# Three centred-only tiles instead of two, one of them in column halves of its product, with all loads on one queue and a newly searched order

## The chip, the cores and the metric

One core of a Trainium2 chip. The rounds ran on several chips (the first comparison on one, e1 to e8 on a second, e9 to e11 on a third, e12 and e13 on a fourth), and each ratio compares runs of the same rounds. The metric is device microseconds of one execution, median of several runs. The span, from the first to the last instruction in a profile, is about 1.3 us shorter than that time. All runs compared here are fast ones with a granted TensorE clock of 1.0.

## The reference

```python
# x: (1, 2048, 512) bf16; w1, w2: (512, 512); w3: (512, 1792); w4: (1792, 512)
h  = gelu(layernorm(x) @ w1)
hs = concat([shift(h_j, s) for h_j, s in zip(split(h, 4), (1, -1, 2, -2))]) @ w2   # zero padded along tokens
x1 = x + hs
out = x1 + gelu(layernorm(x1) @ w3) @ w4
```

## The kernel before

Tokens lie in 16 tiles of 128 rows; in the names, tiles 16 to 31 are those of x1, the input of the second layer norm. A small recording layer collects operations with their reads and writes, a list scheduler in the kernel's source puts them in an order for each engine, and semaphores are derived from that order. Layer 1 needs layernorm(x) with the channels on partitions, so each normalised tile is transposed, by TensorE (`ty`, `sa`/`sb` in the script) or by a DMA transpose. Then 128-column "up" products give h with channels on partitions, ready for the mixing product.

The first two tiles take another path, "centred only" (`NAT`). Only the mean is subtracted before the transpose; the product is made with the tokens on partitions ("rows"), where 1/sigma can be a per-partition scale of the GELU, and h is transposed back (`th`). So TensorE can start before `rstd` (1/sigma) is known.

```python
GROUPS = {1: (1, 1, 1, 1, 1, 1, 2, 2, 2, 2, 2), 2: (2, 2, 4, 4, 4)}
NORM = {4: "act", 5: "act", ...}          # engine of a tile's normalisation; default VectorE
NAT = (0, 1)                              # centred-only tiles
SPLIT = (0,)                              # ... centred and transposed in column halves
LOADS = """
x0 w1a w1b x4-5 w2b tp2 x3 w2a x6-7 w3b x8 w3a x1@act x9 x2@act x11 tp16 w4a x10 tp11 w4b tp9 x12-14 x15
"""
SCRIPT = """
warm:8 sa:0 sb:0 ty:1 ra:0 rb:0 up1:1 ty:2 th:0-1 up1:2 mix:0 ty:4 ty:3 mix:1 up1:3 ty:5 up1:4 mix:2 up1:5
mix:3 ty:17 mix:4 up2:0 up1:6 up2:1 mix:6 down:1 mix:5 up1:7-8 ...
"""

# in ln(): a centred-only tile
if t in SPLIT:
    for hh in (0, 1):
        cs = slice(hh * D // 2, (hh + 1) * D // 2)
        pg.add(how, f"norm{q}_{hh}", ... e.tensor_scalar(dst[:, cs], src[:, cs], mv[:, q, 0:1], None, ALU.subtract))

# in mm_up_rows(t): the product with tokens on partitions
if t in SPLIT:
    for hh in (0, 1):                     # halves of the sum over channels: first half needs w1a and half of x only
        pg.add("pe", f"rows{t}_{hh}", part(2 * hh, 2 * hh + 2), ...)
        if hh == 0:
            yield
pg.add("act", f"gelur{t}",
       lambda e: e.activation(hn[:, k, :], y_ps[:, p, 0:D], ACT_F.Gelu_apprx_tanh, scale=rstd[:, t : t + 1]), ...)

# in ln(), at its end: tiles that TensorE does not transpose
if q not in pe_tp:
    pg.add("sp", f"tp{q}",
           lambda e: e.dma_start(xT[:, :, P * t : P * (t + 1)], xn_buf[:, slot(q), :], transpose=True), ...)
```

`GROUPS` says how many tiles each block of up products takes, for layers 1 and 2. In `LOADS`, `w1a` is the first half of w1, `x4-5` one transfer of two tiles, `@act` a load issued from ScalarE's queue; everything else is issued by SyncE in this order, with the DMA transposes and the stores.

Of the kernel before, what the change touches and what calls it, by code (L numbers as in the profile page):

```python
# [6 lines left out]
P = 128  # L7
# [18 lines left out]
class Program:  # L26
# [5 lines left out]
    DUE = 252723.0  # L32
# [225 lines left out]
GROUPS = {1: (1, 1, 1, 1, 1, 1, 2, 2, 2, 2, 2), 2: (2, 2, 4, 4, 4)}  # L258
NORM = {4: "act", 5: "act", 6: "act", 10: "act", 11: "pool", 12: "pool", 13: "act", 15: "act", 18: "pool", 20: "pool", 21: "pool", 22: "pool", 24: "act", 28: "act", 30: "pool"}
EVAC = {1: "both", 2: "dve", 3: "dve", 7: "both", 9: "dve", 10: "both", 11: "both", 13: "both", 16: "dve", 17: "both", 19: "both", 20: "dve", 22: "both", 23: "dve", 24: "dve", 25: "dve", 28: "dve", 31: "dve"}  # L260
STAT_ACT = (1, 6, 8, 9, 12, 21, 22, 23, 27, 28, 29)
TAIL = (256, 128, 128)
NMR = {0: "pool", 1: "pool", 3: "pool", 5: "pool", 7: "pool", 9: "pool", 10: "pool", 12: "pool", 13: "pool", 14: "pool", 17: "pool", 18: "pool", 19: "pool", 21: "pool", 22: "pool", 23: "pool", 27: "pool", 30: "pool"}
NAT = (0, 1)
SPLIT = (0,)
HEV = {2: "dve", 5: "dve", 6: "dve"}
BIAS = {}
LOADS = """
x0 w1a w1b x4-5 w2b tp2 x3 w2a x6-7 w3b x8 w3a x1@act x9 x2@act x11 tp16 w4a x10 tp11 w4b tp9 x12-14 x15
"""  # L270
SCRIPT = """
warm:8 sa:0 sb:0 ty:1 ra:0 rb:0 up1:1 ty:2 th:0-1 up1:2 mix:0 ty:4 ty:3 mix:1 up1:3 ty:5 up1:4 mix:2 up1:5
mix:3 ty:17 mix:4 up2:0 up1:6 up2:1 mix:6 down:1 mix:5 up1:7-8 mix:8 mix:7 up1:9 mix:10 down:0 down:2 mix:9
up1:10 mix:12 mix:11 up2:2 mix:13 down:3 down:6 mix:14 up2:3 mix:15 down:4-5 down:7 down:11 down:9-10 up2:4
down:8 down:12 down:14 down:13 down:15
"""

def bass_standalone__mixer_s_mlp__prompt_kernel(nc, x, w1, w2, w3, w4, out):
# [14 lines left out]
    with ExitStack() as es:  # L293
# [37 lines left out]
        def pair_rv(p, v):  # L331
            return [(("y", p, 0), v), (("y", p, 1), v)]
# [180 lines left out]
        def mm_up_rows(t):  # L513
# [11 lines left out]

            if t in SPLIT:
# [7 lines left out]
            else:  # L534
# [6 lines left out]
                   reads=pair_rv(p, v) + [(("rstd", t), 0), (("warm",), 1)], writes=[(("hn", t), 0)], dur=50 + D * 0.833)  # L541
            yield

        def h_transpose(t, pair):
            g = group_of[1, t]
            how = HEV.get(t, "act")
            k = NAT.index(t)
            if pair:
                b, v = next_pair()
                res, dst = pair_rv(b, v), y_bf[:, b, 0:D]  # L550
            else:
                b, v = next_bank()
                res, dst = [(("o", b), v)], o_bf[:, b, 0:D]

            def f(e):
                for c in range(DC):
                    ins = e.transpose(dst[:, P * c : P * (c + 1)], hn[:, k, P * c : P * (c + 1)], ident[:])  # L557
                return ins

            pg.add("pe", f"th{t}", f, reads=[(("hn", t), 0), (("ident",), 1)], writes=res, dur=225)  # L560
            to, frm = hT[:, :, 2 + P * t : 2 + P * (t + 1)], dst.rearrange("p (c s) -> p c s", s=P)
            pg.add(how, f"evh{t}",
                   (lambda e: e.activation(to, frm, ACT_F.Copy)) if how == "act" else
                   (lambda e: e.tensor_copy(to, frm)),
                   reads=res, writes=[(("h", j, g), 0) for j in range(DC)],
                   dur=(60 + 0.82 * D) if how == "act" else (75 + 0.51 * D))

# [37 lines left out]
        def run(gen):  # L605
            for _ in gen:
                pass
# [81 lines left out]
        steps = []  # L689
# [4 lines left out]
        steps = [s for s in steps if s[0] not in ("th", "tz") or s[1] in NAT]  # L694
# [13 lines left out]
        for kind, n in steps:  # L708
            if kind == "warm":
                warm_pe(n)  # L710
            elif kind in ("sa", "ra"):
# [118 lines left out]
```

## Time and profile before

| | before |
|---|---|
| time, median (range) | 135.71 us (135.43 to 135.89) |
| profiled span | 134.6 us |
| TensorE busy | 130.6 us |
| first TensorE wait on data | 0.4 us on w1, at 5.6 us |

How to read the views: a chain line is start, length, what; it follows the last instruction back to what released it. A wait line is engine, line and tile of the waiter, what it waited for, total us, times, longest. A timeline line is start, length, engine, line, operation, output and inputs, count. L586 (L619 after the change) are the up products, L655 (L688) the down products, L626 (L659) the mixing products, L520 and L534 the row products, L482 (L483) transposes of x, L557 (L587) transposes of h. PSUM is the buffer that TensorE writes; ScalarE or VectorE must empty a part of it before it is used again.

### The profile page before, as it was taken

To read this page: it belongs to the slowest core of one execution; us is meant where nothing else is said; L and a number is where in the kernel's file an instruction comes from. 1 tells how busy PE (TensorE), PEld (TensorE's weight loads), DVE (VectorE), ACT (ScalarE), POOL (GpSimd) and SP (SyncE) were. 2 spreads that over 40 slices of the span, in tenths; PEclk is the share of its full clock that TensorE was granted. 3 is DMA by queue.
4 is the path that set the end of the run, shared out by engine and by line. 5 is a ranking of instruction groups with operands and counts; after the bars stand their busy time and mean duration, and the time that the engine had idled before them with its cause. 6 is when DMAs were issued, how large, how long until landed. Compare 5 with 4: busy or idle time off the path is not lost.

```text
span 134.6 us, 2013 instructions
## 1 busy us (share of the span) xinstructions
PE 130.6 (97%) x780; PEld 72.7 (54%) x792; DVE 52.1 (39%) x140; ACT 58.5 (44%) x90; POOL 25.9 (19%) x59
## 2 busy tenths in 40 slices
PE   8889999999999999999999999999999999999994
PEld 3467688886586446444444444444444444444463
DVE  3779999403947627700053500062222200012222
ACT  6598995768484402775530366500000155520000
POOL 2533467600865301200010310010000000000000
DMA  6999398599056532111003110003111100001112
GB/s 198 298 381 380 80 294 161 98 271 271 0 117 82 118 78 78 39 39 39 5 0 78 39 39 0 0 0 85 39 39 65 52 0 0 0 5 39 39 39 78
DMA packets 21897, 12.32 MB, mean 92 GB/s; under 512 B 14464, under 2 KB 21376, under 8 KB 21888
## 3 DMA queue, kind: packets, MB, share of 16 engines
q1 hardware_dynamic: 21168, 11.80, 32.9%
q10 hardware_dynamic: 720, 0.39, 1.0%
q8 instruction: 6, 0.10, 0.3%
q14 instruction: 3, 0.02, 0.0%
HBM read 6.82 MB, written 2.10 MB: 66 GB/s over the span
## 4 chain that ended last, share of the span: by engine, by line
PE 93%; DMA 4%; issue 1%; SPq 1%; ACT 1%; DVE 0%; ACTq 0%
PE y_ps L586 45%; PE o_ps L655 36%; PE o_ps L626 10%; DMA w_sb<-in_w_dram 4%; PE y_ps L520 1%; PE y_ps L482 1%; ACT hn L539 1%; SPq L372 0%; PE o_ps L557 0%; SPq L365 0%; DVE o_sb L663 0%; ACTq L779 0%; SPq L815 0%
## 5 line engine op out<-in xcount | busy, mean ns | idle before, releaser
L586 PE MATMUL y_ps<-xnT,w_sb 128*128 128x256 bf16 (+2 forms) x421 | 62.4, 306 | 0.2
L586 PEld LDWEIGHTS y_ps<-xnT,w_sb 128*128 128x128 bf16 x424 | 39.0, 98 | 23.4 <-DVE xnT L490 0.3
L655 PE MATMUL o_ps<-w_sb,h2T 128*128 128x512 bf16 (+2 forms) x247 | 49.0, 355 | 0.3
L601 ACT ACTIVATE h2T<-y_ps 128x1024 bf16<-128x1024 f32 (+1 forms) x29 | 28.6, 994 | 42.6 <-PE y_ps L586 42.6
L655 PEld LDWEIGHTS o_ps<-w_sb,h2T 128*128 128x128 bf16 x252 | 23.6, 98 | 25.2
L663 DVE TENSOR_TENSOR o_sb<-o_ps,x_sb 128x512 bf16<-128x512 f32 (+2 forms) x18 | 11.4, 633 | 40.0 <-PE o_ps L655 39.8
L416 POOL TENSOR_TENSOR rstd<-mv,neghalf 128x1 f32<-128x1 f32 x21 | 11.7, 555 | 42.8 <-DVE mv L411 38.7
L626 PE MATMUL o_ps<-w_sb,hT 128*128 128x512 bf16 x60 | 15.2, 379 | 0.3
L409 DVE BATCH_NORM_STATS2 st<-x_sb 128x6 f32<-128x512 bf16 x21 | 14.2, 676 | 2.1 <-DMA x_sb<-in_x_dram 1.8
L637 DVE TENSOR_TENSOR x_sb<-o_ps,x_sb 128x512 bf16<-128x512 f32 x10 | 6.9, 687 | 12.7 <-PE o_ps L626 12.7
L633 DVE SCALAR_TENSOR_TENSOR x_sb<-o_ps,x_sb 128x512 bf16<-128x512 f32 x6 | 4.1, 690 | 16.8 <-PE o_ps L626 16.7
L601 ACT ACTIVATE hT<-y_ps 128x1024 bf16<-128x1024 f32 (+1 forms) x9 | 7.4, 827 | 6.3 <-PE y_ps L586 6.2
L416 POOL TENSOR_TENSOR rstd<-vpe,neghalf 128x1 f32<-128x1 f32 x11 | 6.0, 551 | 18.8 <-DVE vpe L405 18.7
L626 PEld LDWEIGHTS o_ps<-w_sb,hT 128*128 128x128 bf16 x64 | 6.0, 98 | 5.5
L437 DVE TENSOR_SCALAR xn_buf<-x_sb,mv,rstd 128x512 bf16<-128x512 bf16 x15 | 7.0, 469 | 4.9 <-POOL rstd L416 4.6
L446 ACT ACTIVATE xn_buf<-x_sb,nmr,rstd 128x512 bf16<-128x512 bf16 x8 | 6.5, 813 | 5.1 <-DVE nmr L442 3.2
L393 ACT ACTIVATE junk<-x_sb 128x512 bf16<-128x512 bf16 x11 | 6.9, 624 | 2.7 <-DVE x_sb L633 2.7
L449 POOL TENSOR_SCALAR xn_buf<-x_sb,rstd,nmr 128x512 bf16<-128x512 bf16 x7 | 5.4, 768 | 0.8 <-DVE nmr L442 0.4
L679 PE MATMUL o_ps<-zeros 128*128 128x512 bf16 x8 | 3.6, 631 | 0.6 <-POOLq L815 0.6
L411 DVE BATCH_NORM_AGGREGATE mv<-st 128x2 f32<-128x9 f32 x21 | 4.0, 191 | 0.2
L388 ACT ACTIVATE junk<-x_sb 128x512 bf16<-128x512 bf16 x5 | 3.1, 625 | 0.2 <-DMA x_sb<-in_x_dram 0.2
L482 PEld LDWEIGHTS y_ps<-ident,xn_buf 128*128 128x128 bf16 x28 | 2.3, 111 | 1.3 <-issue 0.5
(35 smaller groups left out, 30.5 us busy)
## 6 DMA issues: line engine op xcount, KB each, us to landing
w_sb<-in_w_dram SPq DMA_DIRECT2D x4, 896.0 KB, 6.8
out_dram<-o_sb SPq DMA_DIRECT2D x15, 128.0 KB, 1.7
w_sb<-in_w_dram SPq DMA_DIRECT2D x4, 256.0 KB, 5.2
x_sb<-in_x_dram SPq DMA_DIRECT2D x7, 128.0 KB, 5.2
x_sb<-in_x_dram SPq DMA_DIRECT2D x2, 256.0 KB, 5.5
xnT<-xn_buf SPq DMA_TRANSPOSE x25, 2.5
x_sb<-in_x_dram SPq DMA_DIRECT2D x1, 384.0 KB, 6.0
x_sb<-in_x_dram ACTq DMA_DIRECT2D x2, 128.0 KB, 3.0
```

The source lines that it names most:

```text
L393: (lambda d: (lambda e: e.activation(d, src, ACT_F.Square, accum_out=sums[:, q, 1:2])))(junk[:, b, :]),
L409: pg.add("dve", f"bnst{q}", lambda e: e.bn_stats(st9[:, q, 0:6], src), reads=rs, writes=[(("st", q), 0)], dur=605)
L416: lambda e: e.tensor_tensor(col(rstd), var, neghalf[:], ALU.pow),
L437: lambda e: e.tensor_scalar(dst, src, mv[:, q, 0:1], rstd[:, q : q + 1], ALU.subtract, ALU.mult),
L446: f = lambda e: e.activation(dst, src, ACT_F.Identity, bias=nmr[:, q : q + 1], scale=rstd[:, q : q + 1])
L449: f = lambda e: e.tensor_scalar(dst, src, rstd[:, q : q + 1], nmr[:, q : q + 1], ALU.mult, ALU.add)
L586: ins = e.matmul(y_ps[:, p, W * i : W * (i + 1)], wsb[:, dc, P * fc : P * (fc + 1)], src[:, dc, P * t0 : P * t0 + W], start=(dc == 0), sto ...
L601: (lambda d, s: (lambda e: e.activation(d, s, ACT_F.Gelu_apprx_tanh)))(dst, ysrc),
L626: ins = e.matmul(dst, hT[:, j, c0 : c0 + P], w2_sb[:, j, :], start=(j == 0), stop=(j == DC - 1))
L637: f = lambda e: e.tensor_tensor(x1_sb[:, t, :], dst, x_sb[:, t, :], ALU.add)
L655: ins = e.matmul(dst, h2T[:, fc, P * t : P * (t + 1)], w4_sb[:, fc, cs], start=(fc == 0), stop=(fc == FC - 1))
L663: (lambda d, c: (lambda e: e.tensor_tensor(o_sb[:, oi, c], d, x1_sb[:, t, c], ALU.add)))(dst, cs),
```

## The change

The intent is to fill TensorE's early idle time: a third tile takes the centred-only path, so that more products are ready before the first rstd; tile 1 is split in halves like tile 0 and its products interleaved with tile 0's; the third tile's product is made in two column halves, so that its first GELU starts earlier. Groups, engines of the side work, loads and script were searched anew, with loads that land late assumed in the search.

```diff
-GROUPS = {1: (1, 1, 1, 1, 1, 1, 2, 2, 2, 2, 2), 2: (2, 2, 4, 4, 4)}
+GROUPS = {1: (1, 1, 1, 1, 1, 1, 2, 2, 2, 4), 2: (2, 4, 4, 4, 2)}
+NORM = {1: "pool", 5: "pool", 7: "pool", ...}            # new table; 14 full tiles and tile 1 on GpSimd
-NAT = (0, 1)
-SPLIT = (0,)
+NAT = (0, 1, 2)
+SPLIT = (0, 1)
+CSPLIT = (2,)
-x0 w1a w1b x4-5 w2b tp2 x3 w2a x6-7 w3b x8 w3a x1@act x9 x2@act x11 tp16 w4a x10 tp11 w4b tp9 x12-14 x15
+tp16 x0-1 x2 x3 w1a w1b x4-5 w2b w2a x6 x7-9 tp2 x12 x10-11 w3b w3a w4a w4b x14 x15 tp8 x13
-warm:8 sa:0 sb:0 ty:1 ra:0 rb:0 up1:1 ty:2 th:0-1 up1:2 mix:0 ...
+warm:9 sa:0 sb:0 sa:1 sb:1 ty:2 ra:0-1 rb:0-1 ra:2 ty:3 th:0 rb:2 th:1 up1:3 ta:2 tb:2 mix:0 ty:4 mix:1 ty:5
+up1:4 mix:2 up1:5 ty:16 mix:3 ty:17 mix:4 up2:0 up1:6 down:0 up1:7 ...
+            if t in CSPLIT:                              # in mm_up_rows
+                for hh in (0, 1):
+                    cs = slice(H * hh, H * (hh + 1))
+                    ... 4 products of 256 columns into one half of y_ps, then gelur{t}_{hh} on that half
+                    yield
 (... h_transpose does a CSPLIT tile in two halves in the same way ...)
```

`tp16` and `tp2` in the new list do nothing, because TensorE transposes these tiles.

More of the change, by code (lines that the diff above doesn't have):

```diff
@@ L31 @@
     LOOK = {"dve": 300.0, "act": 300.0}
-    DUE = 252723.0
+    DUE = 414330.0
     BEGIN = {"sp": 30.0, "act": 150.0, "pe": 400.0, "dve": 150.0, "pool": 450.0}
@@ L256, in place @@
         return out
-GROUPS = {1: (1, 1, 1, 1, 1, 1, 2, 2, 2, 2, 2), 2: (2, 2, 4, 4, 4)}
-NORM = {4: "act", 5: "act", 6: "act", 10: "act", 11: "pool", 12: "pool", 13: "act", 15: "act", 18: "pool", 20: "pool", 21: "pool", 22: "pool", 24: "act", 28: "act", 30: "pool"}
-EVAC = {1: "both", 2: "dve", 3: "dve", 7: "both", 9: "dve", 10: "both", 11: "both", 13: "both", 16: "dve", 17: "both", 19: "both", 20: "dve", 22: "both", 23: "dve", 24: "dve", 25: "dve", 28: "dve", 31: "dve"}
-STAT_ACT = (1, 6, 8, 9, 12, 21, 22, 23, 27, 28, 29)
+GROUPS = {1: (1, 1, 1, 1, 1, 1, 2, 2, 2, 4), 2: (2, 4, 4, 4, 2)}
@@ L262 @@
+NORM = {1: "pool", 5: "pool", 7: "pool", 8: "pool", 9: "pool", 10: "pool", 11: "act", 15: "act", 16: "act", 18: "pool", 19: "pool", 20: "act", 22: "pool", 23: "pool", 24: "pool", 26: "pool", 27: "pool", 28: "pool", 29: "pool", 30: "act"}
+EVAC = {0: "dve", 3: "dve", 5: "dve", 9: "both", 10: "both", 11: "both", 14: "both", 15: "dve", 16: "dve", 17: "both", 18: "dve", 19: "dve", 23: "both", 24: "both", 25: "both", 27: "dve", 30: "dve"}
+STAT_ACT = (1, 2, 8, 12, 13, 18, 24, 26, 27, 29, 31)
 TAIL = (256, 128, 128)
-NMR = {0: "pool", 1: "pool", 3: "pool", 5: "pool", 7: "pool", 9: "pool", 10: "pool", 12: "pool", 13: "pool", 14: "pool", 17: "pool", 18: "pool", 19: "pool", 21: "pool", 22: "pool", 23: "pool", 27: "pool", 30: "pool"}
@@ L264 @@
-NAT = (0, 1)
-SPLIT = (0,)
-HEV = {2: "dve", 5: "dve", 6: "dve"}
+NMR = {2: "pool", 3: "pool", 5: "pool", 6: "pool", 8: "pool", 12: "pool", 14: "pool", 17: "pool", 18: "pool", 20: "pool", 22: "pool", 29: "pool", 30: "pool", 31: "pool"}
+NAT = (0, 1, 2)
+SPLIT = (0, 1)
+CSPLIT = (2,)
+HEV = {3: "dve"}
 BIAS = {}
 LOADS = """
-x0 w1a w1b x4-5 w2b tp2 x3 w2a x6-7 w3b x8 w3a x1@act x9 x2@act x11 tp16 w4a x10 tp11 w4b tp9 x12-14 x15
+tp16 x0-1 x2 x3 w1a w1b x4-5 w2b w2a x6 x7-9 tp2 x12 x10-11 w3b w3a w4a w4b x14 x15 tp8 x13
@@ L270 @@
 """
 SCRIPT = """
-warm:8 sa:0 sb:0 ty:1 ra:0 rb:0 up1:1 ty:2 th:0-1 up1:2 mix:0 ty:4 ty:3 mix:1 up1:3 ty:5 up1:4 mix:2 up1:5
-mix:3 ty:17 mix:4 up2:0 up1:6 up2:1 mix:6 down:1 mix:5 up1:7-8 mix:8 mix:7 up1:9 mix:10 down:0 down:2 mix:9
-up1:10 mix:12 mix:11 up2:2 mix:13 down:3 down:6 mix:14 up2:3 mix:15 down:4-5 down:7 down:11 down:9-10 up2:4
-down:8 down:12 down:14 down:13 down:15
+warm:9 sa:0 sb:0 sa:1 sb:1 ty:2 ra:0-1 rb:0-1 ra:2 ty:3 th:0 rb:2 th:1 up1:3 ta:2 tb:2 mix:0 ty:4 mix:1 ty:5
+up1:4 mix:2 up1:5 ty:16 mix:3 ty:17 mix:4 up2:0 up1:6 down:0 up1:7 mix:5 down:1 mix:6 up1:8 mix:8 mix:7
@@ L276 @@
+up1:9 mix:9-10 up2:1 mix:13 mix:12 up2:2 mix:11 down:3 down:7 down:4 mix:14 up2:3 mix:15 down:2 down:6
+down:11 down:8 down:12 up2:4 down:10 down:5 down:9 down:14 down:13 down:15
 """
@@ L524, in part, with f @@
                 return f
+            if t in CSPLIT:
+                H = D // 2
+                for hh in (0, 1):
+                    cs = slice(H * hh, H * (hh + 1))
+                    def f(e, hh=hh, cs=cs):
+                        for dc in range(DC):
+                            ins = e.matmul(y_ps[:, p, 512 * hh : 512 * hh + H], xnT[:, dc, P * t : P * (t + 1)],
+                                           w1_sb[:, dc, cs], start=(dc == 0), stop=(dc == DC - 1))
+                        return ins
+                    pg.add("pe", f"rows{t}_{hh}", f,
+                           reads=[(("w1", c), 0) for c in range(DC)] + [(("xT", t, c), 1) for c in range(DC)],
+                           writes=[pair_rv(p, v)[hh]], dur=DC * 109.2)
+                    pg.add("act", f"gelur{t}_{hh}",
+                           (lambda a, b: (lambda e: e.activation(a, b, ACT_F.Gelu_apprx_tanh,
+                                                                 scale=rstd[:, t : t + 1])))(
+                               hn[:, k, cs], y_ps[:, p, 512 * hh : 512 * hh + H]),
+                           reads=[pair_rv(p, v)[hh], (("rstd", t), 0), (("warm",), 1)], writes=[(("hn", t, hh), 0)],
+                           dur=50 + H * 0.833)
+                    yield
+                return
             if t in SPLIT:
@@ L540, in mm_up_rows, with h_transpose @@
                                           scale=rstd[:, t : t + 1]),
-                   reads=pair_rv(p, v) + [(("rstd", t), 0), (("warm",), 1)], writes=[(("hn", t), 0)], dur=50 + D * 0.833)
+                   reads=pair_rv(p, v) + [(("rstd", t), 0), (("warm",), 1)],
+                   writes=[(("hn", t, hh), 0) for hh in (0, 1)], dur=50 + D * 0.833)
             yield
-        def h_transpose(t, pair):
+        def h_transpose(t):
             g = group_of[1, t]
@@ L547, in h_transpose @@
             k = NAT.index(t)
-            if pair:
+            if t in CSPLIT:
                 b, v = next_pair()
-                res, dst = pair_rv(b, v), y_bf[:, b, 0:D]
+                steps = [(2 * hh, 2 * hh + 2, [pair_rv(b, v)[hh]], f"_{hh}") for hh in (0, 1)]
+                dst = y_bf[:, b, :].rearrange("p (k x) -> p k x", k=2)[:, :, 0 : D // 2]
+                chunk = lambda c: dst[:, c // 2, P * (c % 2) : P * (c % 2 + 1)]
+                part = lambda c0, c1: dst[:, c0 // 2, :].rearrange("p (c s) -> p c s", s=P)
@@ L551, in h_transpose @@
             else:
                 b, v = next_bank()
-                res, dst = [(("o", b), v)], o_bf[:, b, 0:D]
-            def f(e):
-                for c in range(DC):
-                    ins = e.transpose(dst[:, P * c : P * (c + 1)], hn[:, k, P * c : P * (c + 1)], ident[:])
-                return ins
-            pg.add("pe", f"th{t}", f, reads=[(("hn", t), 0), (("ident",), 1)], writes=res, dur=225)
-            to, frm = hT[:, :, 2 + P * t : 2 + P * (t + 1)], dst.rearrange("p (c s) -> p c s", s=P)
@@ L562, in h_transpose @@
-            pg.add(how, f"evh{t}",
-                   (lambda e: e.activation(to, frm, ACT_F.Copy)) if how == "act" else
-                   (lambda e: e.tensor_copy(to, frm)),
-                   reads=res, writes=[(("h", j, g), 0) for j in range(DC)],
-                   dur=(60 + 0.82 * D) if how == "act" else (75 + 0.51 * D))
+                steps = [(0, DC, [(("o", b), v)], "")]
+                dst = o_bf[:, b, 0:D]
+                chunk = lambda c: dst[:, P * c : P * (c + 1)]
+                part = lambda c0, c1: dst.rearrange("p (c s) -> p c s", s=P)
@@ new lines, in h_transpose, with f @@
+            for c0, c1, res, tag in steps:
+                def f(e, c0=c0, c1=c1):
+                    for c in range(c0, c1):
+                        ins = e.transpose(chunk(c), hn[:, k, P * c : P * (c + 1)], ident[:])
+                    return ins
+                n = c1 - c0
+                pg.add("pe", f"th{t}{tag}", f,
+                       reads=[(("hn", t, hh), 0) for hh in range(c0 // 2, c1 // 2)] + [(("ident",), 1)],
+                       writes=res, dur=56 * n if n < DC else 225)
+                to, frm = hT[:, c0:c1, 2 + P * t : 2 + P * (t + 1)], part(c0, c1)
+                pg.add(how, f"evh{t}{tag}",
+                       (lambda a, b: (lambda e: e.activation(a, b, ACT_F.Copy)) if how == "act" else
+                        (lambda e: e.tensor_copy(a, b)))(to, frm),
+                       reads=res, writes=[(("h", j, g), 0) for j in range(c0, c1)],
+                       dur=(60 + 0.82 * n * P) if how == "act" else (75 + 0.51 * n * P))
+                yield
@@ L693, in bass_standalone__mixer_s_mlp__prompt_kernel @@
             steps += [(kind, n) for n in (range(int(a), int(b or a) + 1) if kind != "warm" else [int(n)])]
-        steps = [s for s in steps if s[0] not in ("th", "tz") or s[1] in NAT]
+        steps = [s for s in steps if s[0] != "th" or s[1] in NAT]
         pe_tp = {n for kind, n in steps if kind in ("tp", "ty", "sa")}
@@ L710, in bass_standalone__mixer_s_mlp__prompt_kernel @@
                 warm_pe(n)
-            elif kind in ("sa", "ra"):
-                halves[kind[0], n] = pe_transpose(n, n, True) if kind == "sa" else mm_up_rows(n)
+            elif kind in ("sa", "ra", "ta"):
+                halves[kind[0], n] = {"s": lambda n: pe_transpose(n, n, True), "r": mm_up_rows,
+                                      "t": h_transpose}[kind[0]](n)
                 next(halves[kind[0], n])
-            elif kind in ("sb", "rb"):
+            elif kind in ("sb", "rb", "tb"):
                 next(halves[kind[0], n])
@@ L717, in bass_standalone__mixer_s_mlp__prompt_kernel @@
                 run(pe_transpose(n % NT, n, kind == "ty"))
-            elif kind in ("th", "tz"):
-                h_transpose(n, kind == "tz")
+            elif kind == "th":
+                run(h_transpose(n))
             elif kind == "mix":
```

## The prediction

> **What bounds the kernel now.** I read the page's busy shares and its row of forty slices first, then the chain of work that ended last in order of time, then the waits of TensorE, and last the instructions of the first 18 us one by one.
>
> ```profile
> span 134.6 us, 2013 instructions
> PE 130.6 (97%) x780; PEld 72.7 (54%) x792; DVE 52.1 (39%) x140; ACT 58.5 (44%) x90; POOL 25.9 (19%) x59
> ...
> PE   8889999999999999999999999999999999999994
> ...
> DVE  3779999403947627700053500062222200012222
> ```
>
> TensorE is full in every slice from the fourth on; VectorE is nearly full in slices 4 to 6 only (10 to 20 us), so it can set the pace only there. The share of 97% flatters: it counts warm-up products on zeros and products at half clock. The chain says more:
>
> ```profile
> 0.99 5.01 DMA w_sb<-in_w_dram
> ...
> 6.04 1.48 PE y_ps L520 x6
> ...
> 7.61 0.70 ACT hn L539
> ...
> 8.35 0.40 PE o_ps L557 x4
> 8.75 0.89 PE y_ps L586 x16
> ...
> 17.58 13.97 PE y_ps L586 x128
> ...
> 132.73 0.02 issue
> ```
>
> The columns are start, length, what. Until 6.0 us the end hangs on the second half of w1 landing; at 7.6 on one GELU; from 8.35 us to 132.7 on TensorE alone, product after product. The 128 products of 256 columns from 17.58 us take 109 ns each, so there is nothing to win in the body, unless products are removed, and the sum of columns is not changed. TensorE's waits confirm it; there are three in the whole run:
>
> ```profile
> PE o_ps L679 <- POOLq L815: 0.6, 1, 0.6
> PE y_ps L520 <- DMA w_sb<-in_w_dram: 0.4, 1, 0.4
> PE o_ps L557 <- ACT hn L539: 0.4, 1, 0.4
> ```
>
> **Idle ledger, before.** I take the start of the first 256-column block of layer 2, 17.58 us, as the mark; both kernels have the same kinds of work before it. Useful TensorE work before the mark, from start-to-start spacings in the trace (215.8 ns for 512 columns, 55.6 ns for 128): 8 row products 1.73, 36 transposes 2.00, 64 up products of 128 columns 3.56, 20 mix products 4.32; sum 11.60 us. Lost: 17.58 - 11.60 = 5.98 us. Nearly all lies before 8.35 us. Only this can shrink.
>
> **What the Trainium skill says.** (1) "TensorE: Matmul & The Clock Gate", Part 1, gives 106.7 and 426.7 ns between starts of 128- and 512-column products while cold, 55.6 and 215.7 ns warm, and a change about 4 us into activity. The trace agrees: the warm-up products start every 427 ns from 0.64 us, transposes at 4.03 us are still 107 ns apart, and from about 4.8 us on the spacing is the warm one. (2) "DMA: Bandwidth & Descriptors", Queues, rings and completion order, says each DMA engine takes turns between the queue rows it has work for, by packet. The trace's packets show this: x2, issued from ScalarE, moves between 2.8 and 3.3 us while SyncE's queue nearly stops, and the w1 half behind it reaches ten engines at 4.3 to 4.6 us, the other six at 5.3 to 6.0. (3) "GPSIMD Engine Reference", specification table, says GpSimd shares its SBUF interfaces with VectorE. The trace agrees:
>
> ```profile
> 19.57 0.77 POOL L449 TENSOR_SCALAR xn_buf<-x_sb,rstd,nmr 128x512 bf16<-128x512 bf16 x1
> 19.68 0.80 DVE L437 TENSOR_SCALAR xn_buf<-x_sb,mv,rstd 128x512 bf16<-128x512 bf16 x1 [0.24 <-POOL rstd L416]
> ```
>
> VectorE's normalisation takes 0.41 us when alone, 0.80 us beside GpSimd's. (4) The table at the head of "TensorE: Matmul & The Clock Gate" also says that ScalarE and VectorE take instructions strictly in order; no row of this trace goes against it, and it matters for the new order below.
>
> **The change part by part.**
> *Work.* Tile 2 leaves the 128-column path (16 products of 55.6 ns, 0.89 us) for 8 row products of 256 columns (8 x 109 = 0.87 us) and gains 4 transposes of its product. Tile 16 (the first x1 tile) is transposed on TensorE instead of by DMA: 4 more. So +8 transposes, +0.44 us. One layer-1 group of four tiles replaces two of two: 16 products fewer, at 2.3 ns of fixed spacing each, -0.04 us. A ninth warm-up product fills time that nothing else could use.
> *Loads.* All x loads now go through SyncE's queue; x0 and x1 are one transfer; x2 and x3 stand before w1. So 1024 KB instead of 896 KB precede the end of w1. In the trace the queue moves about 344 KB per us once running (84 to 90 KB per 250 ns); with no turn-taking dip I estimate x0-1 at 2.7 us, x2 3.05, x3 3.4, w1 halves at 4.2 and 5.0. Before they were x0 2.4, w1 3.9 and 6.0.
> *The new head*, by hand from the trace's durations and the order in each engine's program. Nine warm-up products end at 0.64 + 9 x 0.427 = 4.46 us. Tile 0: bn_stats 2.72, aggregate 3.45, halves subtracted from 3.68 on. Tile 1's halves go to GpSimd from 3.52, about 0.5 us each (between its 0.27 for one column and 0.77 for 512); VectorE beside it is slowed, but still ahead of TensorE. Twelve transposes: four cold, the rest warm, done at 5.3. VectorE empties tile 0's first half at 4.91, then its program has bn_stats of tile 3 (about 0.6 us to the next start), then the second half at 5.73 to 6.02. The interleave covers this: first halves of tiles 0 and 1 at 5.29 and 5.72, second halves at 6.15 and 6.59, then tile 2's first column half 7.02, tile 3's transposes to 7.67. GELU of tile 0 comes after a ScalarE sum of squares and ends at 7.81, so the product's transposes wait 0.19. Then second column half, transposes and up products of tile 3 follow with no gap to 9.85. ScalarE must run, in this order, GELU 0, GELU 1, half GELU 2, copy 0, half GELU 2, copy 1: 7.12 + 3 x 0.6 + 0.38 x 2 + 0.6 gives 10.3 us, so mix 0 waits 0.45.
> From there: 5 mixes 4.32, tiles 4 and 5 1.78, transposes of tiles 4, 5, 16, 17 0.89: 10.3 + 6.99 = 17.3. VectorE's copy for tile 17 ends at about 17.25 by the same reckoning, so it is just in time. **Mark at 17.35 us.**
> *Ledger, after:* work 11.60 - 0.89 + 0.87 + 0.44 = 12.03 (rounded); lost 17.35 - 12.03 = 5.32 us. The head loses 0.66 us less, pays 0.43 us more work: the mark moves by -0.23 us. With -0.04 us later: **-0.27 us**. The tail (three column pieces of the last tile) is unchanged, and the last layer-2 block, now two tiles wide, is followed by down products of other tiles first, as before, so its GELUs stay hidden. 135.56 - 0.27 = 135.3; I lean 0.1 us lower, because the order was searched and my hand order takes every wait at full. **135.2 us.**
>
> **Rivals.**
> A. *The loads bite.* If six DMA engines fall behind again (1 to 1.4 us in this trace), w1's second half lands at about 6.4, row products slip 0.3 us and the gain is gone: about 135.5. Against it: one queue, no turn-taking.
> B. *Transposes by DMA wait behind the weights.* Before, tiles 6 and 7 were transposed between w4's halves; now all of w3, w4, x14 and x15 (about 6.5 MB) are queued ahead. At the rates above they end at about 20.4 us; tile 7's transpose then lands at about 21.7. It is needed at 17.35 + 56 x 0.109 = 23.5 us. A margin of 1.8 us; if the queue is slower by a tenth it is used up, and TensorE would stand for up to 1 us: 136.2.
> C. *VectorE or ScalarE becomes the bound from 8 to 18 us.* VectorE is nearly full there; GpSimd has 14 full normalisations where it had 7 (and tile 1's halves), each able to stretch a VectorE pass by 0.4 us. Two such on the path make the mark 18.1: 136.0.
> D. *The head shrinks more than I reckon*: if ScalarE's copies are quicker and mix 0 does not wait, 0.6 us better: 134.6.
> E. *All of it hidden*: the same waits in other places, 135.6.
>
> **Range and chances.** The whole loss that could be removed is 5.98 us, of which 4.1 us pass before the clock is warm, so 2% (2.7 us) faster is hardly possible. Slower by 2% needs B or C several times over. D and C set the range: 134.3 to 136.1. Faster 0.03, same 0.94, slower 0.03.
>
> **What would show it.** TensorE's waits: none on w1 above 0.2 us; one on a GELU or a ScalarE copy of h before mix 0, 0.2 to 0.5 us. The chain: w1 no longer its first long piece, but VectorE or ScalarE pieces between 5 and 10 us. The first 56 products of 256 columns starting at 17.0 to 17.7 us. No wait on a DMA transpose at 23 us. The second half of w1 landing near 5 us. I am wrong if TensorE has a wait of over 0.3 us after the mark, or if the mark lies outside 16.7 to 18.2 us.

## The result

| | before | after |
|---|---|---|
| time, median of 4 runs | 135.71 us (135.43 to 135.89) | 137.43 us (136.78 to 137.76) |
| ratio | | 1.0123 (95%: 1.0076 to 1.0169) |
| profiled span | 134.6 us | 135.4 us (the fastest of the four) |
| first layer-2 block starts ("the mark") | 17.41 us | 17.84 us |
| last product starts | 132.49 us | 133.37 us |
| time between the two | 115.08 us | 115.52 us |

A ratio here is the mean time of one kernel's fast runs over that of the other's of the same rounds, so it is not quite the ratio of the medians. The changed kernel is slower, by 1.2%, still within 2%, but outside the range of 134.3 to 136.1.

The last three rows come from the trace's record of each product. The prediction read the mark of the kernel before as 17.58 us; that is where the chain's piece begins, which is when the product ahead of it is modelled to end. The first product of the block was issued at 17.41.

The page of the changed kernel:

```profile
span 135.4 us, 2007 instructions
PE 131.9 (97%) x777; PEld 71.1 (53%) x777; DVE 52.3 (39%) x142; ACT 56.7 (42%) x89; POOL 32.6 (24%) x67
...
PE   8899999999999999999999999999999999999994
...
DVE  2879999865764700070004144001522220030422
```

GpSimd has 6.7 us more work and VectorE no less. Nothing else on this page tells why the time is longer. TensorE's waits do:

```profile
PE o_ps L712 <- POOLq L849: 0.6, 1, 0.6
PE y_ps L483 <- POOL xn_buf L428: 0.6, 1, 0.6
PE y_ps L619 <- ACT h2T L634: 0.3, 1, 0.3
```

The waits for w1 and for the GELU are gone, as intended. In their place stands one for GpSimd at the start and one before an up product. The chain of the same run places both:

```profile
0.09 2.78 DMA x_sb<-in_x_dram
...
4.78 0.96 POOL xn_buf L428
...
5.78 0.30 PE y_ps L483 x2
...
6.98 0.62 ACT junk L394 x2
...
7.85 0.62 DVE st L410
...
17.96 5.31 PE y_ps L619 x48
23.27 0.02 issue
23.29 1.03 ACT h2T L634
24.33 0.12 issue
24.45 1.91 PE y_ps L619 x16
```

From 24.45 us on, the chain is TensorE without a break, as in the kernel before. The second wait is attributed to a GELU that ended at 24.32 us. But the up products at 24.45 us (layer 1, tiles 6 and 7) don't read that GELU's result, and the PSUM pair that they write had been emptied by an earlier GELU. What they do read is xnT of tile 7, whose DMA transpose landed at 24.31 us by the trace's landing records. Two releases ended within 10 ns, and the profile chose one. A second profile of the same kernel, below, names the other.

The first wait, seen in the timeline of the changed kernel:

```profile
3.80 1.92 POOL L428 TENSOR_SCALAR xn_buf<-x_sb,mv 128x256 bf16<-128x256 bf16 x2 [2.10 <-ACT junk L389]
3.85 0.70 DVE L428 TENSOR_SCALAR xn_buf<-x_sb,mv 128x256 bf16<-128x256 bf16 x2
4.47 0.47 DVE L434 TENSOR_SCALAR xn_buf<-x_sb,mv 128x512 bf16<-128x512 bf16 x1
```

The two half passes of tile 1 on GpSimd take 0.99 and 0.95 us (0.98 from start to start), where I had put about 0.5 us each. VectorE does such a half in 0.29 us when alone (3.38 us in the kernel before).

The loads, by the trace's landing records (us; all 16 engines done):

| | x0 | w1, 2nd half | w3, all | w4, all | x15 | tile 6 transposed | tile 7 transposed |
|---|---|---|---|---|---|---|---|
| before | 2.40 | 6.00 | 14.21 | 30.44 | - | 21.52 | 22.83 |
| after, estimated | 2.7 | 5.0 | - | - | 20.4 | - | 21.7 |
| after, measured | 2.87 | 6.66 | 16.05 | 21.64 | 22.40 | 22.88 | 24.31 |

SyncE's queue in the changed kernel shows how the transposes come to stand behind the loads:

```profile
10.69 5.19 SPq L366 DMA_DIRECT2D x_sb<-in_x_dram  x2
...
19.04 3.87 SPq L456 DMA_TRANSPOSE xnT<-xn_buf  x3
```

Issuing a 128 KB load takes SyncE 0.4 to 0.6 us in most places; x14 and x15 take 3.19 and 1.96 us, with at least half of w3 and all of w4 not yet landed. Tile 6's transpose is issued at 19.04 us, when tile 6 has been normalised, lands after x15, and tile 7's lands 1.43 us after that.

### The profile page after: what moved, and what is told of

Same layout as the page of the kernel before. It is cut to its first block, busy times and chain, and to the rows that moved or that the text cites. A ratio compares the mean times of both kernels' runs of the same rounds, so it can differ in the third digit from the quotient of the medians.

```text
span 135.4 us, 2007 instructions
## 1 busy us (share of the span) xinstructions
PE 131.9 (97%) x777; PEld 71.1 (53%) x777; DVE 52.3 (39%) x142; ACT 56.7 (42%) x89; POOL 32.6 (24%) x67
## 4 chain that ended last, share of the span: by engine, by line
PE 92%; ACT 2%; DMA 2%; issue 1%; DVE 1%; POOL 1%; DVEq 0%; POOLq 0%; SPq 0%
PE y_ps L619 44%; PE o_ps L688 36%; PE o_ps L659 10%; DMA x_sb<-in_x_dram 2%; PE y_ps L483 1%; ACT h2T L634 1%; POOL xn_buf L428 1%; ACT xnT L491 1%; ACT junk L389 1%; ACT junk L394 0%; DVE st L410 0%; PE o_ps L587 0%; PE y_ps L534 0%; DVE o_sb L696 0%; PE y_ps L587 0%
## 5 line engine op out<-in xcount | busy, mean ns | idle before, releaser
L619 PE MATMUL y_ps<-xnT,w_sb 128*128 128x512 bf16 (+2 forms) x392 | 61.8, 316 | 0.3 <-ACT h2T L634 0.3
L619 PEld LDWEIGHTS y_ps<-xnT,w_sb 128*128 128x128 bf16 x392 | 36.4, 98 | 25.3 <-ACT h2T L634 0.6
L688 PEld LDWEIGHTS o_ps<-w_sb,h2T 128*128 128x128 bf16 x252 | 23.6, 98 | 24.8
L666 DVE SCALAR_TENSOR_TENSOR x_sb<-o_ps,x_sb 128x512 bf16<-128x512 f32 x6 | 4.1, 677 | 31.4 <-PE o_ps L659 31.4
L659 PE MATMUL o_ps<-w_sb,hT 128*128 128x512 bf16 x64 | 15.9, 379 | 0.0
L450 POOL TENSOR_SCALAR xn_buf<-x_sb,rstd,nmr 128x512 bf16<-128x512 bf16 x14 | 10.7, 773 | 1.1 <-DVE nmr L443 0.7
L634 ACT ACTIVATE hT<-y_ps 128x1024 bf16<-128x1024 f32 (+1 forms) x8 | 6.9, 862 | 8.5 <-PE y_ps L619 8.5
L394 ACT ACTIVATE junk<-x_sb 128x512 bf16<-128x512 bf16 x11 | 6.9, 624 | 4.4 <-DVE x_sb L666 4.4
L438 DVE TENSOR_SCALAR xn_buf<-x_sb,mv,rstd 128x512 bf16<-128x512 bf16 x10 | 4.9, 493 | 2.8 <-POOL rstd L417 2.7
L447 ACT ACTIVATE xn_buf<-x_sb,nmr,rstd 128x512 bf16<-128x512 bf16 x5 | 4.1, 813 | 0.8 <-POOL nmr L443 0.7
L443 DVE TENSOR_SCALAR nmr<-mv,rstd 128x1 f32<-128x1 f32 x12 | 2.5, 210 | 3.8 <-POOL rstd L417 3.8
L483 PE MATMUL y_ps<-ident,xn_buf 128*128 128x128 bf16 x32 | 3.1, 219 | 0.7 <-POOL xn_buf L428 0.6
```

Of the source, the lines that this page charges most:

```text
L394: (lambda d: (lambda e: e.activation(d, src, ACT_F.Square, accum_out=sums[:, q, 1:2])))(junk[:, b, :]),
L438: lambda e: e.tensor_scalar(dst, src, mv[:, q, 0:1], rstd[:, q : q + 1], ALU.subtract, ALU.mult),
L450: f = lambda e: e.tensor_scalar(dst, src, rstd[:, q : q + 1], nmr[:, q : q + 1], ALU.mult, ALU.add)
L483: ins = e.transpose(chunk(c), xn_buf[:, slot(q), P * c : P * (c + 1)], ident[:])
L619: ins = e.matmul(y_ps[:, p, W * i : W * (i + 1)], wsb[:, dc, P * fc : P * (fc + 1)], src[:, dc, P * t0 : P * t0 + W], start=(dc == 0), sto ...
L634: (lambda d, s: (lambda e: e.activation(d, s, ACT_F.Gelu_apprx_tanh)))(dst, ysrc),
```

## The experiments

Thirteen runs were made, two of them (e1, e11) without an edit. Except in e10 and e13, the edit is applied after the scheduler has fixed the order of the changed kernel (in e8, of the kernel before), so every other instruction keeps its place on its engine. Theories: **W**, TensorE waits for tile 7's DMA transpose, and its landing is an anchor that decides the end; **G**, GpSimd's half passes lengthen the head; **L**, the loads come late because everything is on one queue; **S**, the loss is spread over the body. One number ties all runs together: from the mark to the last product lie 115.08 us before the change and 115.04 after (16 products fewer), plus 0.22 us for each further tile that TensorE transposes there, plus waits.

| run | mark, us | waits after the mark, us | last product, us | time, median us | ratio to before (95%) |
|---|---|---|---|---|---|
| before | 17.41 | 0 | 132.49 | 135.71 | 1 |
| after | 17.84 | 0.48 | 133.37 | 137.43 | 1.0123 (1.0076 to 1.0169) |
| e1, after again | 17.84 | 0.68 | 133.57 | 136.95 | 1.0115 (1.0081 to 1.0149) |
| e2, tile 1 on VectorE | - | - | - | 137.41 | 1.0132 (1.0101 to 1.0164) |
| e3, two load queues | 17.82 | 0.63 | 133.49 | 136.82 | 1.0091 (1.0062 to 1.0120) |
| e4, x14, x15 late | 17.85 | 0.25 + 1.07 | 134.22 | 137.66 | 1.0159 (1.0131 to 1.0187) |
| e5, tile 7 on TensorE | 17.85 | 0 | 133.12 | 136.60 | 1.0078 (1.0052 to 1.0104) |
| e6, e2 + e3 | 17.17 | 0.99 | 133.20 | 137.12 | 1.0109 (1.0081 to 1.0138) |
| e7, e2 + e3 + e5 | 16.84 | 0.50 | 132.60 | 136.73 | 1.0077 (1.0049 to 1.0104) |
| e8, before, one queue | 18.05 | 0 | 133.13 | 135.88 | 1.0013 (0.9992 to 1.0034) |
| e9, GpSimd with two operations | 18.18 | 0.19 | 133.42 | 136.83 | one run |
| e10, x10 to x15 behind the transposes | 17.96 | 0 | 133.00 | 136.44 | 1.0052 (1.0031 to 1.0074) |
| e11, before again | 16.44 | 0 | 131.52 | 134.93 | one run |
| e12, tiles 6 and 7 on TensorE | 17.54 | 0.67 | 133.71 | 137.34 | 1.0128 (1.0089 to 1.0166) |
| e13, e10 with the early order mended | 17.19 | 0 | 132.22 | 135.72 | 1.0009 (0.9971 to 1.0047) |

Mark, waits and last product are of the profiled run only; a wait is the distance between the starts of two products less the usual 0.109 us (256 columns) or 0.216 us (512).

### e1: the changed kernel again

No edit.

> The changed kernel, nothing edited, for a second profile and its spread. In the first profile TensorE's first 256-column block of layer 2 starts at 17.84 us (17.41 before) and the up products of tiles 6 and 7 then wait until 24.45 us, 0.5 us past the end of that block, just after the DMA transpose of tile 7 landed at 24.31. If that transpose is the cause (theory W), a slower run shows the same wait longer, by what the run is longer. Rival (theory S, the clock or the body): a slower run shows the same head and the same wait, and the extra time is spread over the products. Expected ratio to the kernel before 1.008 to 1.017.

The head was the same to 0.01 us, and the wait 0.2 us longer. TensorE's waits and the chain now name the transfer:

```profile
PE y_ps L619 <- DMA xnT<-xn_buf: 0.5, 1, 0.5
```

```profile
20.35 4.16 DMA xnT<-xn_buf
24.51 0.14 issue
24.65 1.91 PE y_ps L619 x16
```

Tile 7's transpose was issued at 20.35 us and landed at 24.51; the products start 0.14 us later. In the first profile it landed at 24.31 and they started at 24.45. The last product is later by just those 0.20 us. That is theory W, and against S. The longest runs (137.4 to 137.8 us) were not caught in a profile.

### e2: tile 1 centred on VectorE

```diff
+for op in pg.seq:
+    if op.name in ("norm1_0", "norm1_1"):
+        op.eng = "dve"
```

> Tile 1's two halves are subtracted on VectorE (0.29 us each in the kernel before) instead of GpSimd (0.99 and 0.95 us), all orders else frozen. Theory G: these two passes hold TensorE from 5.14 to 5.78 us, so the transposes of tiles 1 and 2 come at about 5.0. But w1's halves landed at 5.98 and 6.67 us, so the first row products can only move from 6.13 to about 6.03: with the loads as they are, gain 0.1 to 0.3 us. Rival: the GpSimd passes are the head's whole loss, gain 0.6 us. If neither, under 0.1 us.

No gain: 1.0132 against 1.0115 for the unedited kernel on the same chip. Its profile fell in a run with a granted clock of 0.564 (span 232.4 us), so its times after the first microseconds say nothing. Its start still shows which release comes last: the twelve transposes run from 4.44 to 5.48 us with no wait on GpSimd, then TensorE waits 0.2 us for w1, whose first half landed at 5.94, and the first row product starts at 5.98 us (6.13 and 6.14 unedited), as expected under G. By itself the time looked like a verdict against G; e6 shows why it isn't one.

### e3: x1 and x2 on ScalarE's queue

```diff
-dma_x0 (SyncE): x_sb[:, 0:2]      dma_x2 (SyncE)
+dma_x0 (SyncE): x_sb[:, 0:1]      dma_x1, dma_x2 (ScalarE), right after it
```

> x0 alone first on SyncE's queue, x1 and x2 on ScalarE's, as before the change; all else of the changed kernel frozen. Theory L: SyncE's queue alone moves almost nothing from 2.9 to 3.5 us while its third transfer is not yet started, and the second queue filled that hole; so every later load lands 0.5 to 0.8 us earlier (w1's second half 6.0 instead of 6.67, x15 21.6 instead of 22.4), tile 7's transpose no later than about 23.7, and TensorE's wait at 24 us goes: gain 0.5 to 1.2 us. Rival (the prediction's own reading, taking turns costs): landings are no earlier and the time is the same within 0.2 us, or longer.

In this profile the early loads did land earlier: w1's second half at 5.97 us instead of 6.66, all of w3 at 15.23 instead of 16.05. The lead was lost again in w4: 15 of its 16 engines had w4's first half at 17.86 us or sooner, the sixteenth at 19.23, and x15 landed at 22.46, tile 7's transpose at 24.43. A 16 KB instruction fetch of 1.12 us, from 16.59 us, falls in that time; that it is on the same engine is not shown. The ratio fell by 0.002, with intervals that overlap, and TensorE's waits still name the transpose:

```profile
PE y_ps L483 <- POOL xn_buf L428: 1.1, 2, 0.6
...
PE y_ps L619 <- DMA xnT<-xn_buf: 0.5, 1, 0.5
```

So L is right about w3 (complete at 15.2 us in three of the four runs with two queues and the unedited plan, 15.8 to 16.1 in all five with one at full clock). For w1 it is not shown: its second half landed at 5.62 to 6.91 us in the six runs of the changed kernel with two queues, and at 6.07 to 6.67 in the five with one. By itself the edit is worth 0.3 us by the ratios, which is within the noise.

### e4: x14 and x15 after the transpose of tile 8

```diff
-dma_w4b dma_x14 dma_x15 tp6 tp7 tp8 dma_x13
+dma_w4b tp6 tp7 tp8 dma_x14 dma_x15 dma_x13
```

> x14 and x15 are issued after the DMA transpose of tile 8 instead of before that of tile 6; all else frozen. Theory W: 256 KB fewer stand ahead, tile 7's transpose lands 0.6 to 0.8 us earlier (about 23.6 us), TensorE's wait before the up products of tiles 6 and 7 goes; gain 0.4 us against the fast runs like the first profile, up to 1.2 us against the slow ones, and a smaller spread. The head does not change (17.84 us). Rival: the wait is on the GELU of layer 2, which the profile names; then nothing changes.

A miss in its time, and a useful one. Tile 7's transpose landed at 24.09 us, only 0.22 us sooner, and the wait there fell from 0.48 to 0.25 us, by as much as the landing moved. But a new and larger wait came, 1.07 us at 31.4 us:

```profile
PE o_ps L688 <- DVE o_sb L696: 0.9, 1, 0.9
```

In VectorE's program the statistics of tiles 14 and 15 stand ahead of the residual sum that frees a PSUM bank, and VectorE stood idle for x14, which landed at 25.43 us:

```profile
25.46 0.69 DVE L410 BATCH_NORM_STATS2 st<-x_sb 128x6 f32<-128x512 bf16 x1 [2.95 <-DMA x_sb<-in_x_dram]
```

The residual sum started at 31.93 us, against 29.41 in the unedited kernel. A load made late held up what stood behind its first reader.

### e5: tile 7 transposed on TensorE

```diff
-tp7: DMA transpose on SyncE
+4 transposes on TensorE between the 2nd and 3rd part of the first layer-2 block, copied out by ScalarE
```

> Tile 7 is transposed on TensorE in the middle of the first layer-2 block (4 transposes, +0.22 us) and copied out by ScalarE, instead of by a DMA transpose that landed at 24.3 to 24.5 us in three profiles; all else frozen. Theory W: the wait of 0.48 to 0.68 us before the up products of tiles 6 and 7 goes (tile 6's transpose landed at 22.9 to 23.1, they are reached at 24.2), so the time falls by 0.25 to 0.45 us to about 136.6, with less spread. Rival (S, the loss is elsewhere): +0.22 us.

As W expects: the mark did not move, the wait is gone, the distance from mark to end is 115.27 us, which is 115.04 and 0.22 for the four transposes, and the ratio falls from 1.0115 to 1.0078. The two intervals overlap, so it is the profile that shows the effect and not the time alone.

### e6: e2 and e3 together

The edit is the two diffs above, of e2 and of e3, in one kernel.

> The edits of the runs e2 and e3 together, so that neither GpSimd nor w1 holds the first row products. Theories G and L: TensorE's first row product starts at 5.1 to 5.4 us instead of 6.13, and the first layer-2 block at 17.1 to 17.5 instead of 17.84. Theory W (the landing of tile 7's transpose at 24.3 to 24.5 us is an anchor): TensorE then only waits longer there, 0.9 to 1.3 us, and the time is that of e3, 136.6 to 137.0 us. Rival (no anchor): the time falls with the head, to 136.2 or lower.

This is the sharpest test of the anchor. The first row product started at 5.52 us instead of 6.13 and the mark came 0.67 us earlier, at 17.17. The last product did not follow; TensorE waited:

```profile
PE y_ps L619 <- DMA xnT<-xn_buf: 0.8, 1, 0.8
```

Tile 7's transpose landed at 24.14 us and the products started at 24.28. The last product came 0.17 us earlier than in the first profile of the changed kernel, by just as much as the landing. A shorter head is worth nothing while that landing stays. It explains e2.

The median, 137.12 us, lies 0.1 us above the expected range. In all six runs the time exceeds the span by about 1.6 us, where the unedited kernel's exceeds it by 1.3; so it is in e7 and e12 (1.6 to 1.7), and in e2 by 1.5. All four have tile 1 moved to VectorE after the order was fixed. Where these 0.2 to 0.4 us (up to 0.003 of a ratio) pass, no trace shows, so these four are better compared by mark and last product than by time.

### e7: e2, e3 and e5 together

The edit is those two and the one of e5.

> The edits of e2, e3 and e5 together. If the head is shortened by 0.4 to 0.7 us and the anchor is gone, the two gains now add: 135.6 to 136.2 us, a wait of under 0.4 us at 23 to 24 us (on tile 6's transpose, landing at 22.9 to 23.1). If the changed kernel's loss lies elsewhere (S), it stays at 136.6 or more.

The expected time was missed by 0.5 us, of which 0.3 lies outside the span (see e6). The mark was at 16.84 us, in part because TensorE's clock was at full speed from its first transposes at 4.16 us on in this run. But now tile 6's transpose, which landed at 23.54 us on the slowest engine, was the anchor; the products started at 23.68. A landing later than the 22.9 to 23.1 us that I had taken from three other runs ate what the head had gained. In e5 it had come late too, at 23.83 us: in both runs with tile 7 off the queue, tile 6's transpose landed 1.1 to 1.3 us after x15, against 0.5 us in the unedited kernel. Why is not known, but taking one transfer away moved its neighbour.

### e8: the kernel before, with x1 and x2 on SyncE's queue

```diff
-dma_x1 (ScalarE) dma_x2 (ScalarE)
+dma_x0 dma_x1 dma_x2 (all SyncE), then w1
```

> The kernel before with one part of the change alone: x1 and x2 on SyncE's queue directly after x0, so that no transfer runs on ScalarE's queue at the start; all else frozen. Theory L: a hole from about 2.9 to 3.5 us opens in which nothing moves, w1's second half lands 0.5 to 0.8 us later than 6.0, and the row products with it: time up by 0.3 to 0.8 us, ratio 1.002 to 1.006. Rival, the prediction's reading (taking turns costs the hole): w1 lands at about 5, time down by 0.4 to 0.9 us.

The same time within 0.2%. w1's second half landed at 5.37 us, so neither expectation held; the half of w2 that is issued last was late instead (9.17 us, against 8.45), and in the profiled run a mixing product waited 0.8 us for a GELU. That run is the longest of the seven (136.50 us), so its mark of 18.05 us is not typical. The load queue alone does not make the kernel before slower.

### e9: GpSimd's half passes with two operations

```diff
-e.tensor_scalar(xn[:, cs], x[:, cs], mean, None, ALU.subtract)
+e.tensor_scalar(xn[:, cs], x[:, cs], mean, 1.0, ALU.subtract, ALU.mult)
```

> The cost of GpSimd's half passes by itself: the same two passes on GpSimd with a second operation (subtract the mean, then multiply by 1.0) in place of the subtraction alone; same result, all else frozen. One subtraction of 128x256 took 0.95 to 0.99 us, while subtract-free normalisations of 128x512 with two operations take 0.77. If the form with one operation is what is slow, the halves take 0.4 to 0.55 us each and TensorE's wait on GpSimd (0.6 us) goes; if it is a 256-column pass or sharing with VectorE that is slow, they stay at 0.9 to 1.0 us. The time in one run says little: 136.5 to 137.7.

My guess about the cost was wrong. The passes took 1.25 and 1.14 us instead of 0.99 and 0.95:

```profile
3.70 2.37 POOL L766 TENSOR_SCALAR xn_buf<-x_sb,mv 128x256 bf16<-128x256 bf16 x2 [2.00 <-ACT junk L389]
```

So the passes with a second operation took 0.2 to 0.3 us more, while a multiply and add over 512 columns takes 0.77 us on the same engine in the same kernel. Why the subtraction is that much dearer per column is not settled; VectorE was at work beside it in these profiles, so sharing is not excluded. The run gave something else: the mark moved back by 0.34 us, to 18.18, and the last product came at 133.42 us, between the two unedited profiles. Tile 7's transpose had landed at 24.36 us, and the products started at 24.50.

### e10: x10 to x15 behind the transposes of tiles 6 and 7

The orders are planned anew with tile 1 on VectorE and this list of loads:

```diff
-tp16 x0-1 x2 x3 w1a w1b x4-5 w2b w2a x6 x7-9 tp2 x12 x10-11 w3b w3a w4a w4b x14 x15 tp8 x13
+x0 x1@act x2@act x3 w1a w1b x4-5 w2b w2a x6 x7-9 w3b w3a w4a w4b tp6 tp7 x10-11 tp8 x12 tp9 x13-14 x15
```

> A version built from the findings, with its orders planned anew: three centred-only tiles kept, tile 1 centred on VectorE, x1 and x2 on ScalarE's queue, and x10 to x15 issued after the transposes of tiles 6 and 7 instead of before. 384 KB fewer stand ahead of w4's end (about 20.6 us instead of 21.7), so by theories W, G and L: tile 6's transpose lands at 21.5 to 22.5 us, tile 7's by 23.3, the first layer-2 block starts at 16.8 to 17.3 us, and TensorE waits under 0.3 us before the up products of tiles 6 and 7. Time 135.0 to 135.7 us, ratio 0.995 to 1.001. If the body holds something else, 136.3 or more.

The anchor is gone: no wait after the mark, 115.04 us to the last product, and six runs within 0.25 us of each other. The time is 0.7 us above what I expected, in the region that I had named for a loss in the body, but the profile puts it in the head: the new plan put VectorE's statistics of tile 3 before tile 2's centring, and TensorE waited 0.9 us for that; w1's halves landed at 6.25 and 6.91 us.

### e11: the kernel before again

No edit.

> The kernel before, nothing edited, for a second profile of it. Its first profile (span 134.6 us) is among its longer runs (133.7 to 134.8). Expected in a shorter one: w1's second half lands before 6.0 us, or TensorE's clock is at full speed before 4.8 us, and the first layer-2 block starts at 16.9 to 17.3 us instead of 17.41, with the same 115.1 us from there to the last product. Rival: the mark is the same and the rest varies.

The chain of the two profiles of the kernel before differs in one respect. At the line where the layer-2 block begins, which started at 17.58 us in the first profile (the line is in the prediction), this one has:

```profile
16.61 13.97 PE y_ps L586 x128
```

w1's second half landed at 4.66 us instead of 6.00, the 0.4 us wait for it is gone, and TensorE's clock was up at its first transposes (3.81 us, against about 4.8). The mark, 16.44 us, is earlier than I had expected (16.9 to 17.3). From it on, the two are alike: 115.08 us. So the head of one kernel varied by 1 us between two runs, and they are near the two ends: the profile that I predicted from was the longest of its four runs (135.89 us; eleven runs on the second chip had spans of 133.7 to 134.8 us, median 134.3, against its 134.6), while e11's 134.93 us lies below all eleven runs of its round (135.27 to 136.02).

### e12: tiles 6 and 7 on TensorE

```diff
 (the edits of e7)
-tp6: DMA transpose on SyncE
+4 transposes of tile 6 on TensorE, copied out by ScalarE behind a GELU of the layer-2 block
```

> As e7 (tile 1 on VectorE, x1 and x2 on ScalarE's queue, tile 7 transposed on TensorE), and tile 6 transposed on TensorE too (+0.22 us of work). No DMA transpose can then hold the up products of tiles 6 and 7. If the head and the two landings are the whole loss: first layer-2 block at 16.8 to 17.3 us, no wait above 0.15 us after it, last product 115.5 us after the mark; time 135.5 to 136.1 us, ratio 1.001 to 1.004. If something else in the body costs time, it stays at 1.0075 like e5 and e7.

A miss that I made myself. TensorE waited 0.67 us for ScalarE's copy of tile 6, which I had put behind a GELU of the layer-2 block:

```profile
PE y_ps L521 <- DMA w_sb<-in_w_dram: 0.6, 2, 0.3
PE y_ps L619 <- ACT xnT L808: 0.5, 1, 0.5
```

The run does not tell what it was made for. Its sum is still right: 115.04 + 0.44 + 0.67 is 116.15, measured 116.17.

### e13: e10 with the early order mended

```diff
-ScalarE: sum of tile 1, squares of tile 1, sum of tile 2     VectorE: ... ev0_0 bnst3 norm2 ev0_1
+ScalarE: sum of tile 1, sum of tile 2, squares of tile 1     VectorE: ... norm2 ev0_0 bnst3 ev0_1
-warm:9
+warm:8
```

> As e10 (x10 to x15 behind the transposes of tiles 6 and 7), with the mean of tile 2 taken before the squares of tile 1 on ScalarE, tile 2 centred before VectorE's statistics of tile 3, and eight warm-up products instead of nine. In e10 TensorE waited 0.9 us for tile 2's centring and 0.2 us for w1. Expected: first layer-2 block at 16.7 to 17.2 us, no wait at 24 us, last product 115.05 us after the mark; time 135.1 to 135.8 us, ratio 0.998 to 1.002. If it is at 1.005 like e10, the head is held by w1 or by another order.

As expected: 135.72 us, ratio 1.0009, and no loss is left that these runs can show (95%: 0.9971 to 1.0047). The chain of this run is TensorE from its first warm-up product to the end, and TensorE's waits are one, the 0.6 us at the very start. The beginning of the chain:

```profile
0.65 3.59 PE o_ps L712 x8
4.24 1.27 PE y_ps L483 x12
5.51 1.88 PE y_ps L521 x8
7.39 0.44 PE y_ps L534 x4
```

The transposes of tiles 6 and 7 landed at 20.46 and 21.09 us, w4's last half at 19.96. Its mark, 17.19 us, lies between the two of the kernel before (17.41 and 16.44). This version keeps the idea of the change and is as fast as the kernel before, not faster. It differs from the changed kernel in loads, queues, tile 1's engine and order at once, so it shows that no loss is left when neither the head nor the landing holds TensorE, and not the share of each change.

## Why the prediction was wrong

**"The new head ... Mark at 17.35 us".** Wrong by 0.49 us (17.84 and 17.84). The mis-sized term is "about 0.5 us each" for GpSimd's halves of tile 1; they took 0.99 and 0.95, and TensorE could not transpose the second half and tile 2 before 5.78 us, where the sum had it done at 5.3. I had interpolated between a one-column pass and a multiply-and-add of 512 columns; the operation here is another one. The estimate of w1's landing (5.0; measured 6.66, 6.64) was wrong too and would have held the head almost as long: the first row product started at 6.13 us with both, at 5.98 without the GpSimd passes (e2, then waiting for w1), at 6.11 with two queues alone (e3), and at 5.52 with both edits (e6). The prediction had 5.29. The predicted wait of 0.45 us before the first mixing product did not come, which took back part of it.

**Rival B, "A margin of 1.8 us".** This is the step that cost the range. The rival named the right wait in the right place, and gave it too small a delay. Tile 7's transpose landed at 24.31 us, not 21.7: the loads end at 22.4 us, not 20.4, and tile 7's landed not 1.3 but 1.9 us after x15. Of the 2.0 us by which the loads are late, 1.7 stood already at w1's second half; e3 and e6 show that gaining them back early is not enough, for w4 lost the lead again. TensorE waited 0.48 and 0.68 us there. The rival's consequence was also missed: such a landing is an anchor, so the head could neither win nor lose time (e6, e9). Even with the mark at 17.35, TensorE would have waited about 1 us for it, which is the 136.2 us of the rival itself; but the top of the range was set by rival C. The prediction's own sign of being wrong, a wait of over 0.3 us after the mark, is what came.

**"With no turn-taking dip".** The hole in the DMA traffic near 3 us was taken for turn-taking between two queues. With one queue it is there too: the trace's packets of the changed kernel show 9 and 6 KB in the two quarter-microseconds from 3.0 us, against 67 to 93 KB from 3.75 to 6.5 us. Its depth varies: the lowest quarter-microsecond between 2.0 and 4.5 us moved 6 to 41 KB in the six profiles with one queue at full clock (41 in e1, where w1 was as late), and 26 to 67 KB in the eight with two. What makes it, and what makes w1 late, stays open.

**The kernel before.** The ledger's 5.98 us of loss counts from 17.58; the product's own start gives 5.81, and e11's run 4.84. Part of what the change was to win was not there in every run. A small misreading stands in the prediction too: VectorE's row has 9 in four slices from 10 to 23.6 us and in one from 34 us, not only from 10 to 20.

**What held.** The later part: -0.04 us for 16 products fewer, measured 115.08 to 115.04. The added work: four transposes are 0.22 us (e5). VectorE's sharing with GpSimd: its half pass at 3.85 us took 0.50 us against 0.29. The chain went through ScalarE and VectorE between 6 and 8.5 us, as foretold, though behind GpSimd. No wait on w1 came, but by luck: w1's second half landed 1.7 us later than estimated and was needed only at 6.99 us, because GpSimd had held TensorE.

**The sum.** Profile against profile: 0.43 us at the mark, 0.48 of wait, -0.04 of work make 0.87; the last product came 0.88 us later. In medians the loss is 1.7 us on the first chip and 1.3 on the second. On the first, 0.2 us more come because the profiled run of the kernel before was its longest (135.89; median 135.71), and 0.65 because that of the changed kernel was its fastest (136.78; median 137.43); what makes its slower runs slower there, no profile caught, and it stays open. On the second chip e1's profiled run is at its median (136.98; 136.95): its last product comes 1.08 us after that of the first profile of the kernel before, whose run was 0.25 us longer than the second chip's median of that kernel, and that makes the 1.3.

## What to carry to other kernels

When one long stream of an engine sets the end, look for the transfers that it must meet on its way: such a landing pins the end, and work won ahead of it turns into waiting, so a single-part undo can look worthless (e2) though it is part of the cure. Before moving loads forward in a queue, list what stands behind them in the same queue and when it is needed, and count the margin with the latest landing seen, not with the mean rate. Take an operation's cost from a row of the same operation on the same engine, and take two profiles before building a ledger on the head of one.

## What the Trainium skill lacked or had wrong

- "GPSIMD Engine Reference", 3.1: its 512-element best case (768 ns predicted, 769 measured) fits this kernel's multiply-and-add of 512 columns (773 ns), and its opening calls VectorE about 2 times faster for elementwise work. A subtraction of a per-partition mean from 256 columns took 945 to 993 ns here, beside work on VectorE, against 286 ns on VectorE alone, so 3.3 to 3.5 times as long, and 1.14 to 1.25 us with a second operation. The page has no figure for this operation.
- "DMA: Bandwidth & Descriptors", DMA Transpose (X-bar): nothing on transposes queued behind loads. Tile 7's landed 1.42 to 1.43 us after tile 6's in the five profiles in which both were queued behind x15 (after, e1, e3, e6, e9), 1.31 us after it in the kernel before, 0.63 us after it in e13, and up to 4.5 us after its own issue (the median of the kernel before's transposes is 2.5 us).
- The same page, Queues, rings and completion order: no figure for what an issue costs when much is still queued. Two 128 KB issues took 3.19 and 1.96 us, with at least half of w3 and all of w4 not yet landed, instead of about 0.45.
- The same page: no word of the dip in traffic after the first transfers of a kernel (9 and 6 KB in two quarter-microseconds of the changed kernel; at the lowest 6 to 41 KB in six profiles with one queue, 26 to 67 KB in eight with two). Turn-taking between queues, which the prediction had made the cause, is not needed for it.
- "TensorE: Matmul & The Clock Gate", Part 4, says that full clock doesn't engage for transposes, as they don't count as busy in the same way. Here transposes ran 55.6 ns apart once the clock was up, and in the first profile of the kernel before it rose at the end of them, at about 4.8 us.
